# Chunked attention with a channel mix on one core: the attention weights are turned after the gate products, and three opening stages get a first product in two halves

## The chip, the core and the metric

The kernel runs on one core of one Trainium2 chip. The metric is the time of one execution on the device in microseconds (us). Five engines work side by side: TensorE (PE in the profile, its weight loads PEld) multiplies matrices into PSUM, VectorE (DVE) and ScalarE (ACT) do elementwise work and read PSUM, GpSimd (POOL) is hardly used, and SyncE (SP) issues nearly all DMAs.

## What is computed

All data are float32: 8 batches, 8 heads, 576 tokens, 64 values per head. Attention works inside chunks of 64 tokens. Its result, with the heads joined to 512 channels, feeds a channel mix with 1024 hidden values.

```
q_c, k_c, v_c = q, k, v reshaped to (B, H, 9, 64, 64)
scores = (q_c @ k_c.T) / 8;  scores -= max(scores)
attn = exp(scores);  attn /= sum(attn) + 1e-9
x = (attn @ v_c), joined to (B, 576, 512)
x_prev = x shifted by one token (zeros ahead of the first)
xk = mu_k * x + (1 - mu_k) * x_prev
xr = mu_r * x + (1 - mu_r) * x_prev
k = relu(xk @ w_k)            # 512 -> 1024
v = (k * k) @ w_v             # 1024 -> 512
out = sigmoid(xr @ w_r) * v   # w_r: 512 -> 512
```

## The kernel before

The 4608 tokens are worked in 18 groups of 256 (two tiles of 128 tokens each, `tl` = 0, 1). A large product is made of three passes over operands that were split into a high and a low part (`PASSES`, L576). The products of a group g on TensorE are:

- **K** (`moe_k`, L593): the hidden values `pk`, four blocks of 24 matmuls with 256 columns, 96 in all. Where g > 3, the first of them is made in two halves of 128 columns, so that the trace counts 97.
- **pt** (`f_tr`, L1037): the attention weights of the next group are turned, eight transposes of 128x128, into a PSUM tile of two banks; ScalarE copies it to `pT` (`f_pT`, L1045).
- **R** (`moe_r`, L647): the gate `pr`, 24 matmuls with 512 columns; ScalarE applies the sigmoid (L661, `sg`).
- **xps** (`f_pv`, L1055): the attention products of the next group, 32 matmuls on 64x64 quarters of the array; ScalarE copies them to `x` (L1081).
- **s** (`group_products`, L970): the scores of the group after the next, 32 matmuls on quarters. The trace has 64 records each for xps and s.
- **V** in groups 0 to 2 (`moe_v`, L678, `pv`, 192 matmuls a group) or, from group 3 on, **W** (`moe_halves`, L867, `vx` and `vyz`, seven blocks of 12 matmuls, since sums of halves take the place of one block).

VectorE makes the maxima, differences and norms of the scores (L998 to L1021), the token mix (L705 `d`, L1117), the low parts (L705, L566) and the sums of halves (`ss`, L813, L705); ScalarE makes the relu and squares (L614, L621), the exponentials (L1007) and the high parts (`kk` L848, L851; `ks` L854).

Nothing schedules this at run time. Two texts of step names give the order in which instructions are written, and each engine works through its own in that order: `START` (groups 0 and 1, the conversion of the weights and the first attention tiles), and `GROUP`, which is run through once for each of the groups 2 to 17. In `GROUP` the step `Pq.0` is the turning, `Pq.1` the copy of `pT`, `Pq.2` the attention products, `Pq.3` and `Pq.4` the start and the copy of `x`, `Nn.0` the scores, `R0.0`, `R1.0` the two gate products, `R0.1`, `R1.1` their sigmoids, `H` and `Z` the high and low parts for W. A mark ahead of a name limits it to some groups.

PSUM has eight banks here: pools `ps_s` (two banks: scores, turned weights), `ps_x` (two: xps, vyz), `ps_k` (two tiles of one bank: pk) and `ps_o` (two of one bank: pr, pv, vx). A new tile of a pool waits until the readers of the tile that had its place are done.

Of the kernel before, what the change touches and what calls it, by code (L numbers as in the profile page):

```python
# [7 lines left out]
F32 = mybir.dt.float32  # L8
# [8 lines left out]
P = 128  # L17
# [35 lines left out]

GROUP = """
Nf.0 K0.0 Lf Sc.0 Sc.1 K0.12 Mr.0 De.0 <De.1 <Lq <Lk Sc.2 K0.3 B.01 K0.4 K1.0 K1.12 E.0 Mr.1 Sc.3456 Mr.2 >De.1 K1.34 K2.0 K2.12 E.1 H.0 K2.34 B.23
K3.0 Pq.0 K3.12 Z.0 Pq.1 K3.34 Z.1 H.1 H.3 Z.2 H.4 Z.3 H.2 H.5 Z.456
R0.0 R1.0 Pq.2 >Nn.0 >Lq >Lk Lv Z.78 R0.1 R1.1 Pq.3 Pq.4 C.0 B.4567 C.2 Md.0 Mk.0 B.8 C.4
V0 V1.0 W.0 W.1 W.2 !W.3 !W.4 W.5 W.6 W.7 Mk.1 W.8 Mk.2 Dl.01 C.1 C.3 V1.12345678 C.5 W.9 W.10 W.12 W.11 ~W.3 ~W.4 W.13 W.14 W.15 W.16
"""

# [19 lines left out]
def tile_chunk_attention_channel_mix(  # L80
# [181 lines left out]
    def quarter(h, c):  # L262

        n = 10 * (h + 1) + c + 1
        if n not in B:
            B[n] = wts.tile([P, 2, HF, HD], F32R, tag=f"b{n}", name=f"b{n}")
        return B[n]
# [314 lines left out]
    def moe_k(g, fp):  # L582
        def f_mm(_):
            pk = T[f"pk{g}{fp}"] = ps_k.tile([P, 2, G], F32, tag="k", name=f"pk_{g}_{fp}")
            xk = T[f"xk{g}"]
            for e in range(2):
                f = 2 * fp + e
                n = 0
                for cb in range(NB):
                    for a, b in PASSES:  # L590
                        parts = tok if g > SPLIT and f == n == 0 else (slice(0, G),)
                        for part in parts:
                            nc.tensor.matmul(  # L593
                                pk[:, e, part],
                                wk[a][:, cb, f * P : (f + 1) * P],
                                xk[b][:, cb, part],
                                start=(n == 0 and part is parts[0]),
                                stop=(n == 3 * NB - 1),
                                skip_group_check=True,
                            )  # L600
                        n += 1

        def f_relu(e):
            if g >= SPLIT:
                if fp == 0:
                    T[f"rr{g}"] = mx.tile([P, NF, G], F32, tag="kk", name=f"rr_{g}", bufs=4)
                r = T[f"rr{g}"][:, 2 * fp : 2 * fp + 2, :]
            else:
                r = mo.tile([P, 2, G], F32, tag="relu", name=f"relu_{g}_{fp}")
            T[f"r{g}{fp}"] = r  # L610
            if e == "D":
                nc.vector.tensor_scalar(r, T[f"pk{g}{fp}"], 0.0, None, ALU.max)
            else:
                nc.scalar.activation(r, T[f"pk{g}{fp}"], AF.Relu)  # L614

        def f_sq(e):
            r = T[f"r{g}{fp}"]
            if e == "D":
                nc.vector.tensor_tensor(r, r, r, ALU.mult)
            else:  # L620
                nc.scalar.activation(r, r, AF.Square)  # L621

        def f_hi(e):
            if f"kk{g}" not in T:
                T[f"kk{g}"] = kk_tiles(g)
            copy(e, T[f"kk{g}"][0][:, 2 * fp : 2 * fp + 2, :], T[f"r{g}{fp}"])

        def f_lo(e):
            hi, lo = (x[:, 2 * fp : 2 * fp + 2, :] for x in T[f"kk{g}"])
            engine[e].tensor_tensor(lo, T[f"r{g}{fp}"], hi.bitcast(F32), ALU.subtract)  # L630

        do.task = f"K{g}{fp}"
        do(f_mm, "P")
        do(f_relu, "A")
        do(f_sq, "A")
        if g < SPLIT:
            do(f_hi, "A")
            do(f_lo, "D")
# [27 lines left out]
    def moe_v(g, tls):  # L666
        do.task = f"V{g}" + "".join(str(x) for x in tls)
        for f in range(NF):

            def f_mm(_, f=f):  # L670
                if f == 0:
                    for tl in tls:
                        T[f"pv{g}{tl}"] = ps_o.tile([P, DM], F32, tag="o", name=f"pv_{g}_{tl}")
                kk = T[f"kk{g}"]
                for tl in tls:
                    for n, (a, b) in enumerate(PASSES):
                        for c in range(2):
                            nc.tensor.matmul(  # L678
                                T[f"pv{g}{tl}"][:, cols[c]],
                                kk[a][:, f, tok[tl]],  # L680
                                quarter(f // HF, c)[:, b, f % HF, :],
                                start=(f == 0 and n == 0 and c == 0),
                                stop=(f == NF - 1 and n == 2),
                                skip_group_check=True,
                            )

            do(f_mm, "P")
        for tl in tls:

            def f_out(_, tl=tl):  # L690
                o = T[f"sg{g}{tl}"]
                nc.vector.tensor_tensor(o, T[f"pv{g}{tl}"], T[f"sg{g}{tl}"], ALU.mult)
                r0 = g * G + tl * TT
                nc.sync.dma_start(out=out_f[r0 : r0 + TT, :], in_=o)

            do(f_out, "D")
# [287 lines left out]
    def group_attention(g):  # L984
# [46 lines left out]
        do.task = f"P{g}q"  # L1031

        def f_tr(_):
            T[f"pt{g}"] = ps_s.tile([P, 2, HP, TT], F32, tag="s", name=f"pt_{g}")
            for tl in range(2):
                for hp in range(HP):
                    nc.tensor.transpose(  # L1037
                        out=T[f"pt{g}"][:, tl, hp, :],
                        in_=T[f"pg{g}"][:, tl, 2 * hp : 2 * hp + 2, :],
                        identity=ident,  # L1040
                    )

        def f_pT(_):
            T[f"pTg{g}"] = att.tile([P, 2, HP, TT], F32, tag="p", name=f"pT_{g}", bufs=1)
            nc.scalar.activation(T[f"pTg{g}"], T[f"pt{g}"], AF.Copy)  # L1045

        def f_pv(_):
            T[f"xps{g}"] = ps_x.tile([P, NB, G], F32, tag="x", name=f"xps_{g}")
# [141 lines left out]
    def group(g):  # L1190
        now, then = ([m for m in range(4, 2 * B_) if load_period(m) == p] for p in (g, g + 1))
        for m in then + now * (g == 2):
            load_blocks(f"m{m}", HB * m, HB)
        if g == 2:
            group_products(g + 1)
        if g + 2 < NG:
            for t in (2 * g + 4, 2 * g + 5):
                load_v(t)
            group_scores(g + 2)
            group_products(g + 2)  # L1200
        if g + 1 < NG:
            group_attention(g + 1)
            group_mix(g + 1)
        for fp in range(NF // 2):
            moe_k(g, fp)
        for tl in range(2):
            moe_r(g, tl)
        split_weights(g)
        if g < SPLIT:
            for tl in range(2):  # L1210
                moe_v(g, (tl,))
        else:
            moe_halves(g)
        steps = late | do.take()
        late.clear()
        late.update({k: v for k, v in steps.items() if k.startswith(f"M{g + 1}r")})
        if g < SPLIT:
            late[f"N{g + 2}.0"] = steps[f"N{g + 2}.0"]
        for k in late:
            del steps[k]  # L1220
        names_of = {
            "Lf": [f"b{nm}m{m}" for nm in "qk" for m in now] * (g == 2),
            "Lq": [f"bqm{m}" for m in then],
            "Lk": [f"bkm{m}" for m in then],
            "Nf": [f"N{g + 1}"] * (g <= SPLIT),
            "Nn": [f"N{g + 2}"],
            "Lv": [f"v{2 * g + 4}", f"v{2 * g + 5}"],
            "De": [f"D{g + 2}e"],
            "Dl": [f"D{g + 2}l"],
            "Sc": [f"S{g + 1}c"],  # L1230
            "Pq": [f"P{g + 1}q"],
            "Md": [f"M{g + 1}d"],
            "Mk": [f"M{g + 1}k"],
            "Mr": [f"M{g}r"],
        }
        for word in GROUP.split():
            if word[0] in "<>":
                if (word[0] == "<") != (g < SPLIT):
                    continue
                word = word[1:]  # L1240
            if word[0] in "!~":
                if (word[0] == "!") != (g == NG - 1):
                    continue
                word = word[1:]
            task, _, numbers = word.partition(".")
            for name in names_of.get(task, [f"{task[0]}{g}{task[1:]}"]):
                which = [numbers] if task == "W" else numbers
                for i in which or range(NF + 1):
                    if f"{name}.{i}" in steps:
                        fn, e = steps.pop(f"{name}.{i}")  # L1250
                        fn(e)
        assert not steps, steps.keys()
# [33 lines left out]
```

## Time and profile before

| | |
|---|---|
| median of 3 runs | 562.27 us (562.17 to 562.47) |
| the profiled execution's own time | 562.54 us |
| its span, first to last instruction | 560.8 us |
| TensorE busy | 554.0 us, 99% |
| VectorE, ScalarE busy | 462.8 us (83%), 346.0 us (62%) |
| TensorE on the chain that ended last | 90% of the span |
| granted clock of TensorE | 1.00 |

The chain that ended last is followed back from the last instruction, at each step to what released it. Durations in the chain are from one link to the next, so links add up; the timeline gives each instruction's own start and length, and pipelined ones overlap. A matmul's length includes its way through the array; in a stream of equal matmuls the distance between starts is what counts.

### The profile page before, as it was taken

How to read it: one execution, taken by the hardware profiler on the slowest of the kernel's cores; microseconds unless marked ns; L12 is line 12 of the kernel's file. 1: busy time of each engine (PE TensorE's matmuls, PEld its weight loads, DVE VectorE, ACT ScalarE, POOL GpSimd, SP SyncE). 2: the span in 40 equal slices, each digit the busy share in tenths (PEclk: the TensorE clock that was granted, in tenths of full speed). 3: DMA queues.
4: the chain of work that ended last, by engine and by line, in shares of the span. 5: the costliest groups of instructions: out<-in, count | busy, mean ns of one | idle time of the engine just before them, and what ended most of it. 6: DMA issues, size and time to landing. Idle time of an engine off the chain costs nothing.

```text
span 560.8 us, 15239 instructions
## 1 busy us (share of the span) xinstructions
PE 554.0 (99%) x6429; PEld 526.6 (94%) x6429; DVE 462.8 (83%) x789; ACT 346.0 (62%) x509; POOL 0.7 (0%) x6
## 2 busy tenths in 40 slices
PE   9999999999999999999999999999999999999997
PEld 8879999999999999999999999999999999999997
DVE  2999999999897889787887978887888788877834
ACT  4899940738475665657565748383929292938461
POOL 0000000000000000000000000000000000000000
PEclk9999999999999999999999999999999999999999
DMA  9998634444443443421243334343343402010011
GB/s 285 272 278 211 133 77 96 69 71 103 67 106 66 96 78 78 66 72 38 57 69 92 65 89 71 87 72 90 62 98 59 106 1 73 6 43 35 3 38 37
DMA packets 184276, 49.24 MB, mean 88 GB/s; under 512 B 169608, under 2 KB 176272, under 8 KB 184208
## 3 DMA queue, kind: packets, MB, share of 16 engines
q1 hardware_dynamic: 183904, 48.01, 38.2%
q8 instruction: 50, 0.82, 0.7%
q10 hardware_dynamic: 304, 0.27, 0.1%
q14 instruction: 18, 0.15, 0.1%
HBM read 38.80 MB, written 9.44 MB: 86 GB/s over the span
## 4 chain that ended last, share of the span: by engine, by line
PE 90%; ACT 7%; DMA 2%; DVE 0%; issue 0%; ACTq 0%
PE pk L593 32%; PE pr L647 16%; PE vx L867 15%; PE vyz L867 11%; PE pv L678 6%; PE xps L1055 3%; PE s L970 3%; PE pt L1037 2%; DMA k_ring<-in_k 2%; PE warm L1183 1%; ACT wk L141 1%; ACT wv_st L295 1%; PE trk L357 1%; ACT wv_st L299 1%; ACT relu L614 0%; ACT wk_st L299 0%
## 5 line engine op out<-in xcount | busy, mean ns | idle before, releaser
L593 PE MATMUL pk<-xkhi,wk 128*128 128x256 f32 (+1 forms) x1166 | 202.1, 276 | 0.2 <-ACT relu L614 0.2
L593 PEld LDWEIGHTS pk<-xkhi,wk 128*128 128x128 f32 x1166 | 176.9, 188 | 0.7 <-ACT relu L614 0.4
L593 PE MATMUL pk<-xklo,wk 128*128 128x256 f32 x576 | 160.0, 278 | 0.1
L593 PEld LDWEIGHTS pk<-xklo,wk 128*128 128x128 f32 x576 | 108.2, 188 | 0.5 <-DVE xklo L566 0.4
L614 ACT ACTIVATE rr<-pk 128x512 f32<-128x512 f32 x60 | 35.3, 588 | 114.4 <-PE pk L593 114.4
L647 PE MATMUL pr<-wr,xrhi 128*128 128x512 f32 x288 | 90.4, 395 | 0.0
L867 PE MATMUL vx<-b,ks 128*128 128x256 f32 x540 | 68.5, 276 | 0.0
L867 PE MATMUL vyz<-b,kk 128*128 128x256 f32 x540 | 68.5, 276 | 0.0
L867 PEld LDWEIGHTS vx<-b,ks 128*128 128x128 f32 x540 | 64.5, 188 | 0.0
L867 PEld LDWEIGHTS vyz<-b,kk 128*128 128x128 f32 x540 | 64.5, 188 | 0.0
L647 PEld LDWEIGHTS pr<-wr,xrhi 128*128 128x128 f32 x288 | 52.7, 188 | 10.3
L647 PE MATMUL pr<-wr,xrlo 128*128 128x512 f32 x144 | 56.2, 390 | 0.0
L896 ACT ACTIVATE u<-vx 128x256 f32<-128x256 f32 x30 | 11.5, 384 | 54.3 <-PE vx L867 54.3
L705 DVE TENSOR_TENSOR kk<-rr,kk 128x1024 fp32r<-128x1024 f32 x30 | 35.4, 1222 | 10.7 <-ACT kk L851 10.6
L621 ACT ACTIVATE rr<-rr 128x512 f32<-128x512 f32 x60 | 38.0, 633 | 1.9
L705 DVE TENSOR_TENSOR xklo<-mk,xkhi 128x1024 fp32r<-128x1024 f32 x15 | 18.4, 1224 | 25.1 <-ACT xkhi L1127 25.1
L678 PE MATMUL pv<-b,kk 128*128 128x256 f32 x288 | 34.7, 280 | 0.0
L678 PEld LDWEIGHTS pv<-b,kk 128*128 128x128 f32 x288 | 33.8, 188 | 0.1
L647 PEld LDWEIGHTS pr<-wr,xrlo 128*128 128x128 f32 x144 | 27.0, 188 | 5.7
L705 DVE TENSOR_TENSOR ks<-ss,ks 128x512 fp32r<-128x512 f32 x45 | 28.3, 684 | 0.0
L1117 DVE SCALAR_TENSOR_TENSOR mk<-d,mu,x 128x256 f32<-128x256 f32 (+3 forms) x80 | 27.7, 413 | 0.4
L1117 DVE SCALAR_TENSOR_TENSOR mr<-d,mu,x 128x256 f32<-128x256 f32 (+3 forms) x80 | 27.5, 410 | 0.0
(119 smaller groups left out, 838.7 us busy)
## 6 DMA issues: line engine op xcount, KB each, us to landing
v<-in_v SPq DMA_DIRECT2D x144, 64.0 KB, 2.6
out<-sg SPq DMA_DIRECT2D x34, 256.0 KB, 2.3
q_ring<-in_q SPq DMA_DIRECT2D x192, 36.0 KB, 2.1
k_ring<-in_k SPq DMA_DIRECT2D x192, 36.0 KB, 2.1
wk_st<-in_moe_w_k SPq DMA_DIRECT2D x4, 1024.0 KB, 9.8
wv_st<-in_moe_w_v SPq DMA_DIRECT2D x4, 1024.0 KB, 7.4
wr_st<-in_moe_w_r SPq DMA_DIRECT2D x2, 1024.0 KB, 8.0
k_ring<-in_k SPq DMA_DIRECT2D x2, 512.0 KB, 7.3
```

What stands on the lines that cost most here:

```text
L593: nc.tensor.matmul(pk[:, e, part], wk[a][:, cb, f * P : (f + 1) * P], xk[b][:, cb, part], start=(n == 0 and part is parts[0]), stop=(n == ...
L614: nc.scalar.activation(r, T[f"pk{g}{fp}"], AF.Relu)
L621: nc.scalar.activation(r, r, AF.Square)
L647: nc.tensor.matmul(pr, xr[a][:, cb, tl * TT : (tl + 1) * TT], wr[b][:, cb, :], start=(n == 0), stop=(n == 3 * NB - 1),)
L678: nc.tensor.matmul(T[f"pv{g}{tl}"][:, cols[c]], kk[a][:, f, tok[tl]], quarter(f // HF, c)[:, b, f % HF, :], start=(f == 0 and n == 0 and c ...
L705: nc.vector.tensor_tensor(to, x, y, ALU.subtract)
L867: nc.tensor.matmul(to, a[i][:, f, :], weight(w, j, f), start=first and f == 0 and n == 0, stop=f == HF - 1 and n == 2, skip_group_check=True,)
L896: nc.scalar.activation(T[f"u{g}"][n // 2][:, n % 2], src(), AF.Copy)
L970: nc.tensor.matmul(T[f"s{g}"][halves[e], j, tl, hp, :], qT[halves[j], hp, cols], kT[halves[j], hp, cols], start=True, stop=True,)
L1037: nc.tensor.transpose(out=T[f"pt{g}"][:, tl, hp, :], in_=T[f"pg{g}"][:, tl, 2 * hp : 2 * hp + 2, :], identity=ident,)
L1055: nc.tensor.matmul(T[f"xps{g}"][halves[c], 2 * j + a, tl * TT + e * CH : tl * TT + (e + 1) * CH], T[f"v{2 * g + tl}"][halves[j], hp, e, :] ...
L1117: nc.vector.scalar_tensor_tensor(out=to[:, cb, s : s + w], in0=T[f"d{g}"][:, cb, s : s + w], scalar=mu[:, cb : cb + 1], in1=T[f"xg{g}"][:, ...
```

## The change

The order table now holds two versions of the middle of a group. Groups 3 to 15 take the words marked `]`, groups 2, 16 and 17 those marked `[`. In groups 3 to 15 the turning stands after both gate products, then come the scores, then the attention products. The PSUM tile of the turned weights is cut into two tiles of one bank from pool `ps_k`, and the copy to `pT` into two instructions. The sigmoid of the first gate half is written ahead of the copies, that of the second behind the copy of `x`. The first matmul of K in group 1, of V in group 0 and of V of the second tile in group 1 is made in two halves of 128 columns with the same weights.

```diff
-K3.0 Pq.0 K3.12 Z.0 Pq.1 K3.34 Z.1 H.1 H.3 Z.2 H.4 Z.3 H.2 H.5 Z.456
-R0.0 R1.0 Pq.2 >Nn.0 >Lq >Lk Lv Z.78 R0.1 R1.1 Pq.3 Pq.4 C.0 B.4567 C.2 Md.0 Mk.0 B.8 C.4
+K3.0 [Pq.0 K3.12 Z.0 [Pq.1 K3.34 Z.1 H.1 H.3 Z.2 H.4 Z.3 H.2 H.5 Z.456
+R0.0 R0.1 R1.0 ]Pq.01 ]Nn.0 Pq.2 >Lq >Lk Lv Z.78 [R1.1 Pq.3 Pq.4 ]R1.1 C.0 B.4567 C.2 Md.0 Mk.0 B.8 C.4
...
-                        parts = tok if g > SPLIT and f == n == 0 else (slice(0, G),)
+                        parts = tok if (g > SPLIT and f == n == 0) or (g, f, n) == (1, 0, 0) else (slice(0, G),)
...
+                            first = f == n == c == 0 and tl == tls[0]
+                            parts = tok if first and (g, tl) in ((0, 0), (1, 1)) else (slice(0, HD),)
+                            for part in parts:
+                                nc.tensor.matmul(
+                                    T[f"pv{g}{tl}"][:, cols[c]][:, part],
+                                    kk[a][:, f, tok[tl]],
+                                    quarter(f // HF, c)[:, b, f % HF, part],
...
-            T[f"pt{g}"] = ps_s.tile([P, 2, HP, TT], F32, tag="s", name=f"pt_{g}")
+            if SPLIT < g < NG - 1:
+                T[f"pt{g}"] = [
+                    ps_k.tile([P, HP, TT], F32, tag="k", name=f"pt{tl}_{g}") for tl in range(2)
+                ]
...
-            nc.scalar.activation(T[f"pTg{g}"], T[f"pt{g}"], AF.Copy)
+            for tl in range(2):
+                nc.scalar.activation(T[f"pTg{g}"][:, tl], T[f"pt{g}"][tl], AF.Copy)
...
+            if word[0] in "[]":
+                if (word[0] == "[") != (g < SPLIT or g + 2 >= NG):
+                    continue
+                word = word[1:]
```

TensorE in group 5, from the last product of K to the second of R, and from the last of R to W. Before:

```order
L593 MATMUL pk_3_2828<-xkhi_2612,wk_119 128x256
L1037 MATMUL pt_2853<-ident,p_2749 128x128 x8
L647 MATMUL pr_0_2883<-wr_120,xrhi_2754 128x512
...
L647 MATMUL pr_1_2896<-wr_120,xrlo_2755 128x512
L1055 MATMUL xps_2909<-pT_2868,v_2591 64x64 x16
L1055 MATMUL xps_2909<-pT_2868,v_2596 64x64 x16
L970 MATMUL s_2942<-kT,qT 64x64 x32
L867 MATMUL vx_3042<-b_918,kk_5_2825 128x256 x2
```

The same place of TensorE after:

```order
L593 MATMUL pk_3_2836<-xkhi_2620,wk_119 128x256
L647 MATMUL pr_0_2880<-wr_120,xrhi_2762 128x512
L647 MATMUL pr_0_2880<-wr_121,xrhi_2762 128x512
...
L647 MATMUL pr_1_2895<-wr_120,xrlo_2763 128x512
L1046 MATMUL pt_6_2908<-ident,p_2757 128x128 x4
L1046 MATMUL pt_6_2909<-ident,p_2757 128x128 x4
L973 MATMUL s_2921<-kT,qT 64x64 x32
L1065 MATMUL xps_2954<-pT_2918,v_2601 64x64 x16
L1065 MATMUL xps_2954<-pT_2918,v_2606 64x64 x16
L870 MATMUL vx_3052<-b_919,kk_5_2833 128x256 x2
```

R now follows K directly, and the turning, the scores and the attention products stand in one piece between R and W.

ScalarE in group 5, from the last square to the copies of `x`. Before:

```order
L621 ACTIVATE rr_2751<-rr_2751 128x512
L1045 ACTIVATE pT_2868<-pt_2853 128x1024
L848 ACTIVATE kk_5_2825<-rr_2751 128x1024
L854 ACTIVATE ks_5_2864<-ss_5_2866 128x512
L854 ACTIVATE ks_5_2864<-ss_5_2870 128x512
L851 ACTIVATE kk_5_2825<-rr_2751 128x4x128
L854 ACTIVATE ks_5_2864<-ss_5_2876 128x512
L661 ACT_TABLE_LOAD
L661 ACTIVATE sg_0_3019<-pr_0_2883 128x512
L661 ACTIVATE sg_1_3021<-pr_1_2896 128x512
L1081 ACTIVATE x_3023<-xps_2909 128x4x192
L1081 ACTIVATE x_3023<-xps_2909 128x4x64
```

The same place of ScalarE after:

```order
L851 ACTIVATE kk_5_2833<-rr_2759 128x1024
L857 ACTIVATE ks_5_2863<-ss_5_2865 128x512
L857 ACTIVATE ks_5_2863<-ss_5_2867 128x512
L854 ACTIVATE kk_5_2833<-rr_2759 128x4x128
L857 ACTIVATE ks_5_2863<-ss_5_2873 128x512
L661 ACT_TABLE_LOAD
L661 ACTIVATE sg_0_2893<-pr_0_2880 128x512
L1055 ACTIVATE pT_2918<-pt_6_2908 128x512
L1055 ACTIVATE pT_2918<-pt_6_2909 128x512
L1091 ACTIVATE x_3031<-xps_2954 128x4x192
L1091 ACTIVATE x_3031<-xps_2954 128x4x64
L661 ACTIVATE sg_1_3036<-pr_1_2895 128x512
```

The copy of `pT` moved from ahead of the high parts to behind the first sigmoid, as two, and the second sigmoid moved behind the copies of `x`. The rows of VectorE and SyncE stand in the same order as before.

## Rows read from the trace of the kernel before

**Rows 1.** The page: busy us (share of the span) xinstructions.
```profile
PE 554.0 (99%) x6429; PEld 526.6 (94%) x6429; DVE 462.8 (83%) x789; ACT 346.0 (62%) x509; POOL 0.7 (0%) x6
```

**Rows 2.** Waits from 94 us on: engine line waited for, us in total, times, longest.
```profile
PEld xps L1055 <- issue: 5.3, 15, 0.4
```

**Rows 3.** The chain in group 5 and its neighbours: start us, us, what.
```profile
171.35 1.09 PE xps L1055 x64
172.44 0.93 PE s L970 x64
173.38 1.57 PE vx L867 x12
...
183.11 11.01 PE pk L593 x97
194.12 0.87 PE pt L1037 x8
```

**Rows 4.** The chain in groups 16 and 17, where later groups' work is missing.
```profile
521.73 1.57 PE vx L867 x12
...
542.46 5.47 PE pr L647 x24
547.93 1.39 PE vx L867 x12
549.32 1.36 PE vyz L867 x12
```

**Rows 5.** The chain in the opening, 52 to 95 us.
```profile
61.80 0.69 ACT relu L614
62.54 3.01 PE pk L593 x24
65.55 5.66 PE pv L678 x48
...
81.69 11.30 PE pv L678 x96
```

**Rows 6.** Timeline of TensorE near 31.8 us: start us, us, engine line op.
```profile
31.57 0.27 PE L464 MATMUL pt<-ident,p 128*128 128x128 f32 x1
31.78 0.33 PE L357 MATMUL trq<-ident,q_ring 128*64 128x128 f32 x2
```

**Rows 7.** Timeline of ScalarE in group 5.
```profile
194.15 0.60 ACT L614 ACTIVATE rr<-pk 128x512 f32<-128x512 f32 x1 [0.70 <-PE pk L593]
...
199.38 1.28 ACT L661 ACT_TABLE_LOAD   x1
200.67 1.08 ACT L661 ACTIVATE sg<-pr 128x512 f32<-128x512 f32 x2
201.64 1.09 ACT L1081 ACTIVATE x<-xps 128x768 f32<-128x768 f32 x2
```

**Rows 8.** Timeline of ScalarE in group 17, which turns no weights.
```profile
542.50 0.60 ACT L614 ACTIVATE rr<-pk 128x512 f32<-128x512 f32 x1 [0.94 <-PE pk L593]
...
546.45 0.63 ACT L854 ACTIVATE ks<-ss 128x512 fp32r<-128x512 f32 x1
```

**Rows 9.** Tile pT, copies of the opening: ns min/median/max, first and last start.
```profile
L141 ACT ACTIVATE pT<-pt x6: 570/593/600, 17.1 to 73.5; 128x512 f32<-128x512 f32 x6
```

**Rows 10.** Timeline of TensorE: start of the second small block, groups 3 and 5.
```profile
143.16 0.65 PE L970 MATMUL s<-kT,qT 64*64 64x64 f32 x32
...
201.37 0.74 PE L970 MATMUL s<-kT,qT 64*64 64x64 f32 x37
```

**Rows 11.** Timeline of VectorE: the opening's end, groups 3 and 9.
```profile
92.33 0.69 DVE L692 TENSOR_TENSOR sg<-pv,sg 128x512 f32<-128x512 f32 x1 [0.35 <-PE pv L678]
...
139.89 0.69 DVE L705 TENSOR_TENSOR ss<-rr,ss 128x512 f32<-128x512 f32 x1
...
309.32 1.22 DVE L705 TENSOR_TENSOR xrlo<-mr,xrhi 128x1024 fp32r<-128x1024 f32 x1
```

**Rows 12.** Stretch of xps, s and the first of W: busy us, PEclk after POOL.
```profile
200.00:203.00 3.00, 3.00 (x136) 2.58 (x135) 3.00 (x6) 2.72 (x5) 0.00 (x0) 1.00 0.47 77
```

More of the change, by code (lines that the diff above doesn't have):

```diff
@@ L677, in f_mm @@
                         for c in range(2):
[L678 to L685, printed above, removed]
+                            first = f == n == c == 0 and tl == tls[0]
[5 more added lines that the diff above has]
+                                    quarter(f // HF, c)[:, b, f % HF, part],
+                                    start=(f == 0 and n == 0 and c == 0 and part is parts[0]),
+                                    stop=(f == NF - 1 and n == 2),
+                                    skip_group_check=True,
+                                )
             do(f_mm, "P")
@@ L1033, in f_tr @@
         def f_tr(_):
-            T[f"pt{g}"] = ps_s.tile([P, 2, HP, TT], F32, tag="s", name=f"pt_{g}")
+            if SPLIT < g < NG - 1:
+                T[f"pt{g}"] = [
+                    ps_k.tile([P, HP, TT], F32, tag="k", name=f"pt{tl}_{g}") for tl in range(2)
+                ]
+            else:
+                x = ps_s.tile([P, 2, HP, TT], F32, tag="s", name=f"pt_{g}")
+                T[f"pt{g}"] = [x[:, tl] for tl in range(2)]
             for tl in range(2):
@@ L1037, in f_tr @@
                     nc.tensor.transpose(
-                        out=T[f"pt{g}"][:, tl, hp, :],
+                        out=T[f"pt{g}"][tl][:, hp, :],
                         in_=T[f"pg{g}"][:, tl, 2 * hp : 2 * hp + 2, :],
```

## The prediction

> **What bounds the kernel now.** The page comes first: TensorE is busy 99% of the span [rows 1]. So a gain must come from fewer or cheaper instructions on TensorE, or from a wait of TensorE itself. The waits from group 2 on come next. None of them has a matmul of a large product waiting; the one entry of TensorE is the weight load of xps, 15 times, 0.35 us each, with no releaser [rows 2]. The chain then gives the price list of one group [rows 3]: it runs on TensorE without a break, K 11.01, turning 0.87, R 5.47 [rows 4], xps 1.09, s 0.93, W 1.57 for its first block and 1.36 for each of the six others [rows 4], 29.10 us in all. Only what is in this list counts; ScalarE and VectorE count where they come too late for it. The opening is read by itself, since its stages run at another pace [rows 5].
>
> **The reordering on TensorE, 13 groups.** Matmul for matmul the work is the same, so what can change is the price of neighbours. Three are in the rows. Entering the small 64x64 products costs 1.09 - 0.93 = 0.16 us: xps after R has it, s after xps has not [rows 3]. Leaving them costs about 0.2: the first block of W takes 1.57 behind s as well as behind xps, against 1.39 straight behind R [rows 3, 4]. The turning stands between full-size products, and R takes 5.47 in group 17 straight behind K [rows 4]; eight transposes at about 0.11 are 0.87, so nothing is paid for its neighbours. After the change a group has one entry and one exit as before; the entry is now from the transposes instead of from R. What that costs no row shows. The lower end is 0, if a transpose lets the small products in for nothing; the upper end is the 0.16 of R, beyond which no entry in the trace goes. The nearest row is a transpose followed by products on half of the array: 0.21 from start to start [rows 6], twice a transpose's own 0.11, so the entry is paid there too. I take 0.16, and the reordering is worth **0.00 us**, with 13 x 0.16 = 2.1 us of gain as its far end.
>
> **ScalarE, the normal group.** TensorE finishes the turning now behind R, so the copies of `pT` lie between the turning and the attention products, with only the scores (0.93 + 0.16 = 1.09 us) as cover. Are they in time? The sums ahead of it are equal, so the second small block starts when it did before, at 201.37 in group 5 [rows 10]; it is now xps. ScalarE ahead of the copies: group 17 has no copy of `pT` and shows the chain as it will be. There the last high part ends at 546.45 + 0.63 = 547.08, 4.58 after the relu of the last K block began [rows 8]. In group 5 that relu begins at 194.15 [rows 7], so the high parts end at 198.73. Then 1.28 for the table and about 0.60 for one sigmoid [rows 7], up to 200.64 with the short gaps between them. The first copy begins some 0.1 sooner, as neighbours on ScalarE overlap in the rows, and takes 0.59 [rows 9]: 201.13. From the end of the relu at 61.80 + 0.69 = 62.49 to the product that waited for it at 62.54 lie 0.05 [rows 5]; so the weights are there at 201.18, **0.19 us ahead** of need. The second copy ends 0.5 later, and the second half of xps starts 0.47 behind the first: also ahead, by 0.17. The copies of `x` (1.09 in group 5 [rows 7]) begin when xps has ended: 201.37 + 0.93 and the way through the array, near 202.5. They end near 203.6. The second block of W, the first to write where xps stood, follows at 201.37 + 0.93 + 1.57 = 203.87, its weight load some 0.1 sooner; that leaves about 0.1. VectorE gets `x` some 0.4 later than before, and behind its mix it waits for ScalarE in any case. So 12 of the 13 groups pay nothing, with little to spare.
>
> R itself moves 0.87 us ahead and needs the low part `xrlo` for its third product. The latest one is in group 9, where it ends at 310.54 [rows 11]; K ends at 194.12 + 4 x 29.10 = 310.52 there [rows 3], and the third product is two of R's steps (2 x 5.47 / 24 = 0.46) further on. No wait. The scores are free of ScalarE now, since the turned weights no longer sit in their banks, but that was no wait before.
>
> **ScalarE, group 3.** Here VectorE still makes low parts of the weights, and its last `ss` ends only at 139.89 + 0.69 = 140.58 [rows 11]. The last high part, which needs it, ends at 141.23 (0.62 plus the handover), not 0.9 sooner than before. Table 1.28, sigmoid 0.60, copy 0.59 less the overlap: 143.63, seen by TensorE at 143.68. The second small block starts at 143.16 [rows 10]. So xps waits **0.52 us**, once; TensorE has no slack later in which to get it back. From below it is 0, if VectorE's row comes sooner than I think.
>
> **The three halved products.** A stage of 96 products costs 8 x 1.36 = 10.88 at the good pace [rows 4]. K with a halved first product takes 11.01 [rows 3], so halving costs 0.13. V of the second tile in group 1 takes 11.30 without it [rows 5]: 0.42 of slow pace. If the halving does for V what K shows, 11.30 becomes 11.01, **-0.29**. V of group 0 takes 5.66 for its 48 products up to the first turning; 5.44 + 0.13 = 5.57, **-0.09**. K of group 1 would also give 0.09, but behind its 48 products TensorE waits for a relu of ScalarE that ends at 62.49 with ScalarE busy ahead of it [rows 5]; the cover is that wait, and the gain is 0. What comes behind the earlier end of V: the scores and group 2's first K, whose low part follows a VectorE row that itself waited for V (0.35 us, [rows 11]) and moves along. I take -0.38; the ends are +0.26, if two halvings cost and bring no pace, and -0.47, if the third counts too.
>
> The Trainium skill, "TensorE: Matmul & The Clock Gate", section LDWEIGHTS, says that a weight load takes a time set by its columns, and so the same for a halved product; by it each halving is a pure loss of one load (estimate from that page: 0.11 us, 0.32 for three, and a sum of +0.84). K's row shows that loss (0.13) and the pace behind it.
>
> **The sum.** 0.00 + 0.52 - 0.38 = +0.14 us. Against the profiled execution's own 562.54 that is 562.68; the median stands 0.27 below it, so **562.4 us**. A measurement of this kernel can tell about 0.2% (1.1 us) from no change, and this is far inside.
>
> **Rivals.**
>
> *Cheap entry.* The transposes are short, and the small products may slip in behind them for less. For: what is in flight is a 128-column product in place of a 512-column one. Against: rows 6, and the same 0.16 ahead of quite different neighbours. It gives 562.4 - 2.1 = 560.3, half of it 561.4. Chance 0.12. The Trainium skill, "TensorEngine Tiling (Array Packing)", section Key Properties, says that changing the tiling mode drains TensorE; by that rule the entry from the transposes is paid in full, and rows 6 agree (0.21 against 0.11).
>
> *Late weights, the slower side.* The cover of 1.09 us for the turned weights is too short in every group, because the copies start later than I work out, or because the first attention product has to wait for both copies. It decides from 0.19 us on. If both have to be waited for, each group loses 0.5 - 0.2 = 0.3 us, and 12 groups 3.6: 566.0. For: the slack is small and rests on one group that has no table load. Against: the copies go into two halves of `pT`, and each half of xps reads one. Chance 0.12.
>
> *The halving brings no pace in V.* +0.26 in place of -0.38: 563.1. V has two products for each weight tile where K has one, so the likeness is not complete. Chance 0.09.
>
> *Group 3 does not wait.* 561.9. Chance 0.05.
>
> *The clock falls.* Turning, scores and attention products make one stretch of 2.9 us without full-size products, where 2.0 were. In that stretch the granted clock was 1.00, which is 2.4 GHz [rows 12]. If it fell to 1.2 GHz in it, 2.9 us would double in 13 groups: +38 us, 600. Chance 0.02. The Trainium skill, "TensorE: Matmul & The Clock Gate", Part 4, says that transposes do not count as work for the clock in the way that matmuls do; by that rule the longer stretch is a risk. No row here shows a clock below 1.00.
>
> **How the numbers follow.** The forecast has 0.60, the rivals 0.12, 0.12, 0.09, 0.05 and 0.02. Faster by over 0.2% (under 561.15): the cheap entry where it is more than half there, 0.12. Slower by over 0.2% (above 563.4): late weights and the clock, and some of the halving's case together with more than 0.52 in group 3, 0.15. Within 0.2%: 0.73. The range runs from 561.0, which takes in half of the cheap entry, to 563.8, which takes in late weights of 0.1 us a group; what lies outside is 0.2 at most.
>
> **What would show it.** In the chain after: R straight behind K, then turning 0.87, s 1.09, xps 0.93 and the first block of W 1.57, and 29.10 us from group to group, with group 3 alone at 29.6. On TensorE's weight loads one wait for `pT`, about 0.5 us, in group 3. V of the second tile in group 1 at about 11.0 in place of 11.30, and the wait for the relu at 62.5 longer by 0.09. I am wrong if s behind the turning takes 0.93 to 1.0 (cheap entry), if xps waits for ScalarE in group after group (late weights), or if V stays at 11.3.

## The result, and the profile after

The changed kernel takes 567.5 us (567.15 to 569.45, six runs) where the kernel before takes 562.37 beside it (562.17 to 563.0, six runs): a ratio of 1.0094, with 95% interval 1.0079 to 1.0109. It is slower by 5.1 us, and the forecast of 562.4 was wrong. The span grows from 560.8 to 565.7 us, and TensorE is still busy for 99% of it, with three instructions more than in [rows 1]. The page, busy us by engine:

```profile
PE 558.9 (99%) x6432; PEld 532.0 (94%) x6432; DVE 462.9 (82%) x789; ACT 352.0 (62%) x524; POOL 0.7 (0%) x6
```

So, but for one wait in group 3 (below), nothing stands still longer; TensorE takes longer over the same work. The chain in group 5 and its neighbours (start us, us, what; the listing ends within the last line) answers to [rows 3] (`pk` is K, `pr` R, `pt` the turning, `s` the scores, `xps` the attention products, `vx` and `vyz` W):

```profile
183.65 11.02 PE pk L593 x97
194.67 5.47 PE pr L647 x24
200.15 0.87 PE pt L1046 x8
201.02 1.09 PE s L973 x64
202.11 0.93 PE xps L1065 x64
203.04 1.61 PE vx L870 x12
204.65 1.41 PE vyz L870 x12
...
211.72 1.42 PE vx L870 x12
213.14 2.97 PE pk L593 x26
```

In the same place of the kernel before:

```profile
202.49 1.57 PE vx L867 x12
204.06 1.36 PE vyz L867 x12
...
212.22 11.01 PE pk L593 x97
```

K, R, the turning and both small blocks cost what was forecast. W does not: its first block takes 1.61 where it took 1.57, and each of the six others 1.41 where it took 1.36. That is 117.8 ns from product to product ((211.72 - 204.65) / 60) where it was 113.3 (1.36 / 12). From K to K a group takes 213.14 - 183.65 = 29.49 us, and 29.11 before (212.22 - 183.11, [rows 3]): 0.38 more, in 13 groups 4.9. The same shows in the length that the trace gives the products of the tile `vyz` from group 4 into group 15 (up to 500 us; ns min/median/max), in the kernel before and in the changed one; every one is 5 ns longer, not some of them:

```profile
L867 PE MATMUL vyz<-b,kk x420: 276/276/276, 174.8 to 498.9; 128*128 128x256 f32 x140
```
```profile
L870 PE MATMUL vyz<-b,kk x402: 281/281/281, 175.0 to 499.9; 128*128 128x256 f32 x134
```

In groups 16 and 17, which keep the old order, W is as in [rows 4] (chain, changed kernel):

```profile
526.46 1.57 PE vx L870 x12
528.03 1.36 PE vyz L870 x12
...
552.66 1.38 PE vx L870 x12
554.04 1.36 PE vyz L870 x12
```

The opening, which answers to [rows 5]:

```profile
61.42 0.69 ACT relu L614
...
62.16 3.00 PE pk L593 x24
65.16 5.56 PE pv L681 x49
...
81.21 11.00 PE pv L681 x97
```

The two halved products of V do what was forecast (5.57 and 11.01). ScalarE's relu comes 0.38 earlier than in [rows 5], which is chance: in the kernels below, K behind it begins anywhere between 62.1 and 62.9, with the halvings as without them. Group 3, with the one wait of a weight load for `pT` (chain, then the row of the waits from 94 us on: us in total, times, longest):

```profile
141.75 0.60 ACT sg L661
142.35 0.49 ACT pT L1055
...
142.89 1.19 PE xps L1065 x64
144.07 1.61 PE vx L870 x12
```
```profile
PEld xps L1065 <- ACT pT L1055: 0.5, 1, 0.5
```

The stretch from K to W in group 3 is 0.60 longer than before (20.07 for 19.47), a little more than this wait.

So of the three terms of the sum two came out, and the third, the reordering at 0.00, is 4.9 us.

### The profile page after: what moved, and what is told of

Read it like the earlier page. It is cut to its first block, busy times and chain, and to the rows that moved or that the text cites. A ratio compares the mean times of both kernels' runs of the same rounds, so it can differ in the third digit from the quotient of the medians.

```text
span 565.7 us, 15236 instructions
## 1 busy us (share of the span) xinstructions
PE 558.9 (99%) x6432; PEld 532.0 (94%) x6432; DVE 462.9 (82%) x789; ACT 352.0 (62%) x524; POOL 0.7 (0%) x6
## 4 chain that ended last, share of the span: by engine, by line
PE 86%; ACT 7%; SPq 3%; DMA 2%; DVE 1%; issue 1%; ACTq 0%
PE pk L593 31%; PE vx L870 15%; PE pr L647 15%; PE vyz L870 11%; PE pv L681 6%; PE s L973 3%; PE xps L1065 3%; PE pt L1046 2%; DMA k_ring<-in_k 2%; SPq L199 2%; ACT wk L141 1%; SPq L291 1%; SPq L184 1%; ACT wv_st L295 1%; ACT wv_st L299 1%
## 5 line engine op out<-in xcount | busy, mean ns | idle before, releaser
L870 PE MATMUL vx<-b,ks 128*128 128x256 f32 x540 | 70.7, 280 | 0.0
L870 PE MATMUL vyz<-b,kk 128*128 128x256 f32 x540 | 70.6, 280 | 0.0
L870 PEld LDWEIGHTS vx<-b,ks 128*128 128x128 f32 x540 | 66.5, 189 | 0.0
L870 PEld LDWEIGHTS vyz<-b,kk 128*128 128x128 f32 x540 | 66.5, 189 | 0.0
L681 PE MATMUL pv<-b,kk 128*128 128x256 f32 (+1 forms) x290 | 34.3, 278 | 0.0
L708 DVE TENSOR_TENSOR d<-x 128x1024 f32<-128x1024 f32 (+3 forms) x20 | 18.8, 958 | 14.4 <-ACT x L1091 14.3
```

What stands on the lines that cost most here:

```text
L681: nc.tensor.matmul(T[f"pv{g}{tl}"][:, cols[c]][:, part], kk[a][:, f, tok[tl]], quarter(f // HF, c)[:, b, f % HF, part], start=(f == 0 and ...
L708: nc.vector.tensor_tensor(to, x, y, ALU.subtract)
L870: nc.tensor.matmul(to, a[i][:, f, :], weight(w, j, f), start=first and f == 0 and n == 0, stop=f == HF - 1 and n == 2, skip_group_check=True,)
```

## What the experiments were to find

What slows W's 84 products in the 13 groups? In the list of instructions, W's surroundings differ in three ways: the attention products stand ahead of it and no longer the scores; its first product no longer waits for ScalarE (it needs the bank that the first sigmoid frees, and the attention products have already waited for the later copies); and the turned weights have other banks and two copies. "Quick" below is a W with blocks of 1.36 us behind its first, "slow" one with 1.41. The pace of each kernel is read from one traced execution. T is the turning, S the scores, A the attention products, t an unread turning; a number in brackets counts products.

### What stands right ahead of W

**Scores first, old turning.** One word moved in the kernel before:

```diff
-R0.0 R1.0 Pq.2 >Nn.0 >Lq ...
+R0.0 R1.0 >Nn.0 Pq.2 >Lq ...
```

> The kernel before with one thing moved: the scores of the next group but one stand ahead of the attention products, and the turning of the weights, the copies pT and the first sigmoid stay where they were. So W follows the attention products, as in the changed kernel, but its first product still carries its wait for ScalarE (the bank that the first sigmoid frees). Theory A (the block ahead of W sets the pace): W at 117.8 ns a product, blocks of 1.61 and 1.41 us, 562.4 + 13 x 84 x 0.0045 = about 567.3 us. Theory B (the wait on W's first product sets the pace): blocks of 1.57 and 1.36 us, 562.4 us. Theory C (it is the banks of the turned weights or the split copies): as B, 562.4 us.

Measured: 562.62 us, ratio 1.0002 (0.9993 to 1.0011). The chain:

```profile
201.19 0.93 PE xps L1055 x64
202.13 1.58 PE vx L867 x12
203.70 1.36 PE vyz L867 x12
```

W is quick behind the attention products. Theory A falls.

**No wait ahead of W.**

```diff
-            T[f"X{g}"] = ps_o.tile([P, HD], F32, tag="o", name=f"vx_{g}")
+            T[f"X{g}"] = (
+                ps_k.tile([P, HD], F32, tag="k", name=f"vx_{g}")
+                if SPLIT <= g < NG - 2
+                else ps_o.tile([P, HD], F32, tag="o", name=f"vx_{g}")
+            )
```
(that is, in groups 3 to 15)

> The kernel before in its old order, with one thing changed: in groups 3 to 15 the tile vx of W takes a bank of the pool of K's products, which ScalarE has long read, and no longer the bank that the first sigmoid frees. The scores still stand directly ahead of W, but W's first product has no wait left; the third still waits for VectorE. Theory A (the block ahead): blocks of 1.57 and 1.36 us, 562.4 us. Theory B (the missing wait): 1.61 and 1.41 us, 562.4 + 4.9 = about 567.3 us. Theory C (banks of the turned weights or split copies): 562.4 us.

Measured: 562.4 us, ratio 0.9999 (0.9990 to 1.0009); blocks of 1.57 and 1.36. Theory B falls as it stands.

**Sigmoid behind the copies.**

```diff
-R0.0 R0.1 R1.0 ]Pq.01 ]Nn.0 Pq.2 ...
+R0.0 [R0.1 R1.0 ]Pq.01 ]R0.1 ]Nn.0 Pq.2 ...
```

> The changed kernel with ScalarE's first sigmoid of groups 3 to 15 written behind the two copies pT instead of ahead of them. TensorE's order is that of the changed kernel (scores, attention products, W), but W's first product gets its wait for ScalarE back, since the sigmoid is now ScalarE's later work; it ends about 0.3 us ahead of W (copies end at 201.6 at the earliest, sigmoid 0.6 us, W at 203.0). Theory A (the block ahead): W stays at 1.61 and 1.41 us, 567.5 us. Theory B (the wait): 1.57 and 1.36 us, 567.5 - 4.9 = about 562.6 us; if a wait that is already met does nothing, 567.5 us with W as it was. Theory C (banks or split copies): 567.5 us.

Measured: 576.96 us, ratio 1.0254 (1.0238 to 1.0269). The chain shows what the expectation overlooked: ScalarE loads its table for the sigmoid (1.28 us) behind the copies now, and W stands still for it.

```profile
201.87 1.09 ACT pT L1055 x2
...
202.98 1.28 ACT L661
...
204.27 0.61 ACT sg L661
...
204.92 1.65 PE vx L870 x12
206.57 1.36 PE vyz L870 x12
```

Dearer, but W is quick after that stop. It settles nothing on a wait that is already met.

**W's first product halved.**

```diff
+                    opening = w == 11 and f == n == 0 and SPLIT <= g < NG - 2
+                    parts = tok if opening else (slice(0, HD),)
+                    for part in parts:
...
-                        to,
+                            to[:, part],
...
-                        weight(w, j, f),
+                            weight(w, j, f)[:, part],
```

> The changed kernel with one thing added: in groups 3 to 15 the first product of W is made in two halves of 128 columns, as the change does in the opening stages and as K's first product is made in groups 4 to 17. If the pace of W is set at its first products and a halved one brings the quick pace, the 84 products go from 117.8 to 113.3 ns, less about 0.1 us for one more product in each stage: 567.5 - 13 x (0.38 - 0.1) = about 563.9 us, blocks after the first of 1.36 us. If the quick pace comes from the wait alone (theory B in its narrow form) or W is slow for another reason (its operands, the copies beside it), the halves only add 13 x 0.06: about 568.3 us.

Measured: 564.33 us, ratio 1.0031 (1.0021 to 1.0042): 3.2 us come back. The chain:

```profile
202.87 1.68 PE vx L873 x13
204.55 1.36 PE vyz L873 x12
```

With the same operands, copies and neighbours W is quick. So a change of its first product alone is enough to set its pace, which it then keeps, and that pace is the loss.

### Both at once, and what else is near

**Scores first and no wait**, the two single edits together in the kernel before:

> The kernel before with the two single edits of the first runs together: the scores ahead of the attention products, and vx in a bank of K's pool, so that W follows the attention products and its first product has no wait. The turning, its banks, the single copy pT and the sigmoids are the old ones. Theory D (W falls into the slow pace only where it follows the attention products and its first product has no wait, both at once): blocks of 1.61 and 1.41 us in groups 3 to 15, 562.4 + 13 x 0.38 = about 567.3 us. Theory C (it takes the new banks of the turned weights or the split copies): blocks of 1.57 and 1.36 us, 562.4 us.

Measured: 562.71 us, ratio 1.0006 (0.9996 to 1.0016); blocks of 1.58 and 1.36. Theory D falls, and this seems to leave C, the banks or the copies.

**The half in which the small products end.** In the first of these two kernels the scores of the kernel before, with `vx` in the other bank, are made forward; in the second the attention products of the changed kernel have their halves turned round:

```diff
-            back = -1 if g > SPLIT else 1
+            back = 1
```
```diff
-                        for c in range(2):
+                        for c in (0, 1)[::back]:
```

> The kernel before with vx in a bank of K's pool (no wait on W's first product; W stayed quick with that alone) and with the scores made in forward order in all groups, so that their last products fill the upper half of the output partitions, as the last attention products do; in the kernel before they are made backwards and end in the lower half. Theory E (without a wait, it is the half in which the last small products end that sets W's pace): blocks of 1.61 and 1.41 us, about 567.3 us. Theory F (scores ahead of W are harmless in either order; something else in the attention products does it): 1.57 and 1.36 us, 562.4 us.

> The changed kernel with one loop of the attention products turned round in the 13 reordered groups: the two halves of the output partitions in the order 1, 0 instead of 0, 1, so that the last products end in the lower half, as the scores do in the kernel before. The same 64 products, no wait added. Theory E (the half of the last small products): W back to 1.57 and 1.36 us, 567.5 - 4.9 = about 562.6 us. Theory F: W stays at 1.61 and 1.41 us, 567.5 us.

Measured: 562.3 us (ratio 0.9996, 0.9987 to 1.0006), W quick; and 567.47 (1.0087, 1.0071 to 1.0103), W slow in 12 of the 13 groups (quick in group 3). Theory E falls.

**Low part first**, so that W's first product has a wait, long met:

```diff
+                turned = w == 11 and f == 0 and SPLIT <= g < NG - 2
+                passes = ((1, 0), (0, 0), (0, 1)) if turned else PASSES
```

> The changed kernel with the first three products of W in another order in the 13 reordered groups: the one with the low part of the activations, which waits for VectorE (its producer ends at 201.1 us where W starts at 203.0), goes first instead of third. The same products; only now W's first product carries a wait, one that has long been met. Theory G (any wait on the first product does, met or not): W at 1.57 and 1.36 us, about 562.6 us. Theory H (it has to be a wait that stops TensorE, or one that leaves the third product's wait in its place as well): W at 1.61 and 1.41 us, 567.5 us.

Measured: 567.28 us, ratio 1.0088 (1.0072 to 1.0104); W slow in groups 5 to 15, quick in 3 and 4. A met wait does not bring the quick pace, at least in 11 of 13 groups.

**Second sigmoid early, and the bank of `vx`** in the changed kernel:

> The changed kernel with ScalarE's second sigmoid of the 13 reordered groups back ahead of the copies x of the attention products, as in the kernel before (it now runs behind them, from 204.1 us in the sixth group). It ends about 0.2 us ahead of the attention products' end, so nothing waits. Theory K (what ScalarE does while W begins sets its pace): W quick, 562.6 us. Theories I and J with banks or copies: W stays slow, 567.5 us.

> The changed kernel with vx in a bank of K's pool in the 13 reordered groups, as in the run of the kernel before with scores first whose W stayed quick although its first product had no wait; that bank was one difference between the two. Theory L (the bank of vx): W quick, 562.6 us. Else W stays at 1.61 and 1.41 us, 567.5 us.

Measured: 567.57 (1.0090, 1.0076 to 1.0103) and 567.46 (1.0088, 1.0074 to 1.0102); W slow in both. Theories K and L fall.

### What stands far ahead of W

**The turning between R's two tiles:**

```diff
-R0.0 R0.1 R1.0 ]Pq.01 ]Nn.0 Pq.2 ...
+R0.0 R0.1 [R1.0 ]Pq.01 ]R1.0 ]Nn.0 Pq.2 ...
```

> The changed kernel with the turning of the weights (pt, 8 products, in the new banks, with the two copies) written between R's two tiles of 128 rows instead of behind the second, in the 13 reordered groups. ScalarE's order is the same; what stands ahead of W on TensorE is now R, scores, attention products, W, without a wait on W's first product, as in the kernel whose W stayed quick. Theory I (the turning standing between R and the scores is what brings W to the slow pace): blocks of 1.57 and 1.36 us, 567.5 - 4.9 = about 562.6 us. Theory J (the new banks, the two copies or the order of the sigmoids): blocks stay at 1.61 and 1.41 us, 567.5 us.

Measured: 563.63 us, ratio 1.0017 (1.0008 to 1.0027). The chain in group 5, and in group 17:

```profile
194.59 2.75 PE pr L647 x12
197.35 0.87 PE pt L1046 x8
198.22 2.73 PE pr L647 x12
...
202.98 1.58 PE vx L870 x12
204.56 1.36 PE vyz L870 x12
...
548.70 1.41 PE vx L870 x12
550.11 1.41 PE vyz L870 x12
```

W is quick in all 13 groups, with the new banks, the two copies and the new order of ScalarE in place: theory J falls. In the traced execution some 0.4 of the 1.0 us above the expectation is the last group: its W is slow here, though its order is the same as in the changed kernel, where it is quick.

**Three products of R behind the turning:**

```diff
-R0.0 R0.1 R1.0 ]Pq.01 ]Nn.0 Pq.2 ...
+R0.0 R0.1 R1.0 ]Pq.01 ]R1.2 ]Nn.0 Pq.2 ...
```
(`R1.2` is the last three of the second tile's 12 products.)

> The changed kernel with the last three of R's 24 products moved from ahead of the turning to behind it (0.68 us of 512-column products between the turning and the scores) in the 13 reordered groups; all else, ScalarE's order too, is that of the changed kernel. Theory M (what counts is what the scores directly follow: the turning's 128-column products bring W to the slow pace, R's 512-column products to the quick one): W at 1.57 and 1.36 us, and the total that of the run with the turning between R's tiles, about 563.6 us. Theory N (the turning has to be further ahead, or ScalarE's copies done earlier): W at 1.61 and 1.41 us, 567.5 + 13 x 0.08 = about 568.5 us.

Measured: 568.03 us, ratio 1.0095 (1.0078 to 1.0112). The chain:

```profile
194.64 4.79 PE pr L650 x21
199.43 0.87 PE pt L1049 x8
200.30 0.70 PE pr L650 x3
...
203.03 1.61 PE vx L873 x12
204.64 1.41 PE vyz L873 x12
```

W is slow in 12 of the 13 groups (quick in group 3), although the scores follow R.

**Eight unread transpositions between R and the small products**, first in the kernel with scores first and no wait, then in the kernel before:

```diff
+        def f_idle(_):
+            for tl in range(2):
+                x = ps_k.tile([P, HP, TT], F32, tag="k", name=f"it{tl}_{g}")
+                for hp in range(HP):
+                    nc.tensor.transpose(
+                        out=x[:, hp, :], in_=T[f"pTg{g}"][:, tl, hp, :], identity=ident
+                    )
```

> The kernel with the scores first, the turning in its old place and vx in K's pool (W was quick in it, 562.7 us), with one thing added in groups 3 to 15: eight transpositions of the turned weights, whose result nobody reads, between R and the scores, in two banks of K's pool. No copy follows them. They cost 0.87 to 0.95 us a group by themselves. Theory M (the eight 128-column products directly ahead of the small ones do it by themselves): W at 1.61 and 1.41 us, 562.7 + 13 x (0.9 + 0.38) = about 579.5 us. Theory N (it takes the copies, the banks' readers or the waits that follow them): W at 1.57 and 1.36 us, 562.7 + 13 x 0.9 = about 574.5 us.

> The kernel before in its own order (attention products, scores, W with its wait for the first sigmoid) with the same eight unread transpositions added between R and the attention products in groups 3 to 15. If they set W's pace through 128 small products whatever their order and whether or not W's first product has a wait: W at 1.61 and 1.41 us, 562.4 + 13 x (0.9 + 0.38) = about 579 us. If the scores directly ahead of W, or the wait, undo it: 1.57 and 1.36 us, about 574.1 us.

Measured: 573.94 us (two runs; ratio 1.0197, 1.0176 to 1.0217) and 574.52 (two runs; 1.0207, 1.0187 to 1.0227), what the transpositions cost by themselves. The chain of the first:

```profile
201.97 0.87 PE it L1099 x8
...
204.87 1.57 PE vx L867 x12
206.44 1.36 PE vyz L867 x12
```

From R on, TensorE's order here is that of the changed kernel, R, T, S, A, W, and W is quick. Theory M falls on both sides. What this kernel has and the changed one lacks is the turning between K and R.

**Four unread transpositions between K and R**, in the changed kernel:

```diff
-R0.0 R0.1 R1.0 ]Pq.01 ...
+Pq.5 R0.0 R0.1 R1.0 ]Pq.01 ...
```
(`Pq.5` turns the identity four times into a bank of `ps_k`.)

> The changed kernel with four transpositions of the identity, whose result nobody reads, added between K and R in the 13 reordered groups, where the kernel before turns its weights. From R's first product on, TensorE's order is that of the changed kernel. They cost some 0.5 us a group themselves. Theory P (the pace of W is carried on from the stage that R follows: straight behind K, whose last stop is 11 us back, R and all behind it start so that W becomes slow; with 128-column products between K and R, W becomes quick): blocks of 1.57 and 1.36 us, 567.5 + 13 x (0.5 - 0.38) = about 569.1 us. Theory Q (what decides lies behind R: ScalarE's copies of the turned weights or the waits of the attention products for them): blocks of 1.61 and 1.41 us, 567.5 + 13 x 0.5 = about 574 us.

Measured: 568.97 us (two runs; ratio 1.0109, 1.0089 to 1.0129; the expectation was 569.1). The chain:

```profile
194.76 0.44 PE it L1104 x4
195.19 5.48 PE pr L647 x24
200.67 0.87 PE pt L1046 x8
...
203.57 1.57 PE vx L870 x12
205.15 1.36 PE vyz L870 x12
```

W is quick in all 13 groups; the copies and the order from R on are those of the changed kernel. The unread tile only shifts, by one in each group, which of the two banks of `ps_k` the later tiles get, and W is quick with either. That everything from R on comes 0.44 us later is not the reason: with the turning between R's tiles, W began 8.39 us behind R's start (202.98 - 194.59), in the changed kernel 8.37 (203.04 - 194.67), and it was quick there. So it is the missing transposes between K and R, some 8 us ahead, that let W fall to the slow pace.

**R's first product halved** instead:

```diff
+                    whole = tl or n or not SPLIT <= g < NG - 2
+                    for part in (slice(0, DM),) if whole else (slice(0, HD), slice(HD, DM)):
```

> The changed kernel with R's first product made in two halves of 256 columns in the 13 reordered groups; the order is that of the changed kernel. Theory P (W's pace is carried on from R's entry): a halved product breaks what K hands to R as it does at the entry of K and V, W at 1.57 and 1.36 us, 567.5 + 13 x (0.06 - 0.38) = about 563.3 us. Theory Q: W at 1.61 and 1.41 us, 567.5 + 13 x 0.06 = about 568.3 us.

Measured: 567.93 us, ratio 1.0089 (1.0072 to 1.0106); W is slow in all 13 groups, with 1.61 for the first block and 1.41 behind it. A halved product does not do at R's entry what it does at those of K, V and W.

### The halvings alone

The kernel before with the three halved products, nothing moved:

> The kernel before with the three halved first products alone, and nothing reordered. As predicted for this part: V of the first group's first tile in 5.57 us instead of 5.66, V of the next group's second tile in 11.01 us instead of 11.30, K of that group behind ScalarE's relu: 562.4 - 0.38 = about 562.0 us. If the quicker pace only makes the next stage wait longer: 562.4 us.

Measured: 561.94 us (561.57 to 562.8) beside 562.52 for the kernel before, ratio 0.9992, interval 0.9983 to 1.0000. This is the best of all versions here, by about what the prediction gave to this part, and at the edge of what can be told from no change. The traces tell it more finely: from the first V of group 0 to the K of group 3 it takes 58.93 us in all 12 kernels with the halvings, and 59.34 to 59.39 in the seven without.

### The runs together

| kernels | on TensorE from K to W, groups 3 to 15 | W |
|---|---|---|
| before; no wait; scores forward; halvings alone | K T R A S W | quick in 13 of 13 |
| scores first, with and without the wait | K T R S A W | 13 of 13 |
| idle transpositions behind R, two kernels | K T R t S A W, K T R t A S W | 13 of 13 |
| idle transpositions ahead of R | K t R T S A W | 13 of 13 |
| turning between R's tiles | K R(12) T R(12) S A W | 13 of 13 |
| changed; second sigmoid early; `vx` in `ps_k`; R halved | K R T S A W | none of 13 |
| attention halves turned; low part first | K R T S A W | 1 (group 3); 2 (groups 3, 4) |
| three products behind the turning | K R(21) T R(3) S A W | 1 (group 3) |

The two kernels whose W stands still or is halved at its start (both K R T S A W) are left out: W is quick there for that reason. Group 16 keeps K T R A W in every kernel, and is quick in all 19. Group 17 has K R W in every kernel, with no turning at all: its W is quick in 10 and slow in 9, the kernel before and the changed one among the 10. So transposes between K and at least the last 12 products of R went with the quick pace without exception; all or nearly all of R straight behind K leaves W to fall either way, mostly to the slow one. Of the four quick exceptions three are in group 3, quick in 3 of the 7 kernels of the last three rows; in groups 4 to 15 it is 1 of 84. Group 3 is the one where xps stands still (0.5 us), and its K is not halved; which of the two matters no run tells.

## Why the prediction was wrong

**The step that failed** is the first term, "the reordering is worth 0.00 us". It was built on "matmul for matmul the work is the same, so what can change is the price of neighbours", and neighbours were taken to be the blocks that touch. The prices of these were right: s behind the turning 1.09, xps behind s 0.93, the turning 0.87, R 5.47. For the way out into W only the first block was compared (1.57 behind s and behind xps, [rows 3, 4]), and the six others were carried over at 1.36. But the rows had shown stages of 96 equal products at two paces, V in 11.30 us [rows 5] and K in 11.01 with a halving in it [rows 3], and the prediction used this for V's halving: "0.42 of slow pace". A stage whose surroundings change could take that pace as well. By those rows that is 84 x 0.42 / 96 = 0.37 a group and 4.8 us in 13, against 4.9 measured. So the rival on the slow side was in the rows and was not named; the term went from 0.00 to a gain of 2.1 us, and had no loss in it.

The row on which W's first block behind xps rested, 521.73 in [rows 4], was the wrong likeness besides: group 16 turns its weights between K and R, which the reordered groups no longer do. The runs show that this is what counts. Group 17, the other row ([rows 4], 549.32), has no turning, and its W was quick there; the later kernels show it at either pace.

**What was right.** The three halvings: V at 5.56 and 11.00 us for 5.57 and 11.01, K of group 1 hidden behind the relu, and by themselves 0.6 us less (the interval goes from 0 to 1.0; 0.41 to 0.46 in the traces), for 0.38. Group 3's wait: 0.5 for 0.52. ScalarE's slack in the other 12 groups: no wait of xps for `pT` in any. The entry from the transposes into the small products costs in full what the entry from R does (1.09), so the cheap entry did not come; nor did late weights, nor a lower clock (granted clock 1.00).

**The sum again**, with the missed term and what the traces give for the other two: 13 x 0.38 + 0.60 - 0.41 = 5.1 us, which is the measured difference.

**What stays open.** How TensorE keeps a pace, and how what stands between K and R reaches W through R and 128 small products, no run shows. A stop of TensorE further up is not enough: in group 3 of the changed kernel xps stood still for 0.5 us and W behind it was slow all the same, as in three more of the seven kernels in the last three rows; that the three others were quick there leaves open whether it plays a part. Nor is it settled how many products of R must stand behind the transposes: 12 were enough and three were not. And the break between K and R was made only with transposes and with a halved product, of which the second did nothing; any other short product, or a pause, was not tried there.

## What to carry to other kernels

A stage of many equal products has a pace as well as a price for its entry, and a change of order has to be priced for both: five ns on each of 84 products in 13 groups outweighed all that was worked out to the tenth of a microsecond. Where a trace shows equal streams at two paces, each stage whose predecessors change gets the other pace as a rival, its products times the difference, also where the blocks that touch it stay alike. If a stage falls to the slow pace, halving its first product, or leaving a few transposes between the long stages ahead of it, is cheap to try; the length that the trace gives one product (276 or 281 ns here) tells at a glance which pace it has.

## What was unexpected of the hardware

- Streams of 256-column products run from start to start at 113.3 or at 117.8 ns, with nothing between, at a granted clock of 1.00; this holds for every stretch of K, V and W in the 19 traces of 24 products or more without a stop. A stage falls into one of the two within its first eight products and keeps it; a W stayed slow through all its seven blocks, and the K behind it, whose first product is halved, was quick again (11.02). The Trainium skill, "TensorE: Matmul & The Clock Gate", section Back-to-back issue gap, says that the distance of products in a stream is set by weight load and product together, and gives one figure for a number of columns; the rows here show two for one and the same code.
- The pace depends on what stood some 8 us earlier. Four transpositions whose result nobody reads, put between K and R for 0.44 us, took 0.36 us a group off W (10.10 to 9.74 by the chain, from its first block to the next K).
- The same order of instructions in group 17 ran at one pace in ten kernels and at the other in nine, in one traced execution of each, though all edits were in other groups. One group's W is worth some 0.36 us, too little to be seen in the times of the other runs; whether the pace belongs to the kernel or changes from execution to execution is open.
